# Three float32 half buffers instead of two, causal masks partly in place, row sums finished on ScalarE, twelve undivided score jobs

## The chip, the cores and the metric

The kernel runs on one core of one Trainium2 chip. The metric is device microseconds of one execution, lower being better; the program before took 1104.03 us (median of three runs, 1100.83 to 1107.71).

## What is computed

An attention with decay feeds two dense layers. Cut to what matters:

```python
B, H, S, D = 4, 8, 576, 64                     # attention: q, k, v; f in (0.8, 1)
scores = q @ k.T / 8 + (cum[:, None] - cum[None, :])   # cum = cumsum(log f)
attn   = softmax(where(causal, -1e9, scores))  # sum + 1e-9 in the divisor
x      = (attn @ v) as (2304 tokens, 512)
h = x @ w_in;  x = (h * clip(h + 3, 0, 6) / 6) @ w_out      # layer 1, 512 -> 2048 -> 512
h = x @ w_in2; x = where(h>=1, h, where(h<=-1, 0, (h+1)**2/4)) @ w_out2   # layer 2
```

The weights come in as 64-bit floats and are turned into float32 on the chip. Matrix products of the dense layers run in three passes on pairs (high part, low part) of a 32-bit format that TensorE reads in one pass.

## The kernel before

**Attention.** The 576 rows of a batch are cut into a first piece (rows 0 to 255) and a second one (256 to 575). `ORDER` lists the eight (batch, piece) in order, the first pieces of batches 0, 1 and 2 first. Each is worked in pairs of heads. For a first piece a pair is one job of kind `two` (two heads, two row tiles of 128); for a second piece it is two jobs of kind `one` (one head, row tiles 2 and 3) and one of kind `last` (64 rows of both heads). So jobs 0 to 11 are of kind `two`. A job goes through `u_load` (DMA from SyncE's queue, two jobs ahead), `u_split` (one job ahead), `u_scores` (scores on TensorE, then `softmax`: VectorE adds the decay and takes the row minimum, ScalarE takes the exponential and sums the row), `u_norm` (1/sum on VectorE, the product on VectorE or ScalarE), `u_trans` and `u_out`.

Jobs below `NATS` (8) are undivided: their q and k (tiles `kn`, `qn`) are loaded as they are and the scores are float32 matmuls over 64 rows (L376). The other jobs load q and k twice over (`kraw`, `qraw`, one buffer each), ScalarE rounds both (`kk`, `qh`), VectorE takes the remainders (L129: the lower half of `kk`, and `ql`), and the scores are two one-pass matmuls over 128 rows each (L386).

The causal mask: GpSimd's affine select (L312) writes the diagonal blocks of the decay tile `dec` into `dm`. A row tile that has columns left of its diagonal block takes two VectorE instructions per head, one on `dec` and one on `dm` that goes on from the first one's minimum.

**Dense layers.** Layer 1 works on token tiles of 256, as steps of one weight chunk each: `moe_h` (12 matmuls, L556, then `u` and `g` on ScalarE and VectorE) and, two steps later, `moe_o` (12 matmuls, L603). Attention pieces are woven between them by planned costs. Layer 2 runs after all attention (L556, L610).

**Weights.** `w_split` turns half a chunk of 64-bit words into float32 in a tile `wr` of tag "wr" (two buffers): ScalarE's L178 starts it, four VectorE instructions (L179, L183, L186, L189) finish it. For layer 1 it is then rounded into place (L196, L197); the halves of layer 2's 16 chunks (`wf16` to `wf31`) are written to memory by a DMA from GpSimd's queue (L194) and read back later. The output tiles `osb` of both layers (L617 to L630) are of the same tag "wr", so they share these buffers. The halves and their times are planned in `wq`; the instructions of each engine are then put in order by a scheduler, and each engine and each queue works in that order.

Of the kernel before, what the change touches and what calls it, by code (L numbers as in the profile page):

```python
# [8 lines left out]
F32 = mybir.dt.float32  # L9
F32R = mybir.dt.float32r  # L10
I32 = mybir.dt.int32
AF = mybir.ActivationFunctionType
ALU = mybir.AluOpType
# [3 lines left out]
P = 128  # L17
# [6 lines left out]
NEG = -8.0e9  # L24


QA = 256
# [1 line left out]
ORDER = ((0, 0), (1, 0), (2, 0), (0, 1), (1, 1), (3, 0), (2, 1), (3, 1))  # L29

DECS = 3
NATS = 8
NORMS = 12
FIRST = 10
EARLY = 6
# [39 lines left out]
def tile_kernel(  # L75
# [10 lines left out]
    nc = tc.nc  # L86
# [3 lines left out]
    moe = ctx.enter_context(tc.tile_pool(name="moe", bufs=2))  # L90
# [19 lines left out]
    att = att_cm.__enter__()  # L110
# [53 lines left out]
    def w_split(kind, c, half, s, raw):  # L164
        if kind == "parts":
            return
        if kind == "whole":
            lo = wsb[s][:, 1]
            rounded("a", wsb[s][:, 0], lo.bitcast(F32))
            rest("v", lo, lo.bitcast(F32), wsb[s][:, 0])  # L170
            return
        ks = slice(4 * half, 4 * half + 4)
        r = moe.tile([P, 4, P], F32, tag="wr", name="wr", bufs=2)
        rf = r.rearrange("p k n -> p (k n)")
        t = rf.bitcast(I32)
        lw, hw = raw[:, :, 0], raw[:, :, 1]

        nc.scalar.activation(out=rf, in_=hw.bitcast(F32), func=AF.Abs)  # L178
        nc.vector.tensor_scalar(  # L179
            out=rf, in0=rf, scalar1=2.0 ** -15, scalar2=122880.0,  # L180
            op0=ALU.max, op1=ALU.min,
        )
        nc.vector.tensor_scalar(  # L183
            out=t, in0=t, scalar1=5, scalar2=2, op0=ALU.logical_shift_left, op1=ALU.logical_shift_right
        )
        nc.vector.scalar_tensor_tensor(  # L186
            out=t, in0=hw, scalar=-1073741824, in1=t, op0=ALU.bitwise_and, op1=ALU.bitwise_or
        )
        nc.vector.scalar_tensor_tensor(  # L189
            out=t, in0=lw, scalar=29, in1=t,  # L190
            op0=ALU.logical_shift_right, op1=ALU.bitwise_or,
        )
        if s is None:
            nc.gpsimd.dma_start(out=wf[c][:, ks], in_=r)  # L194
        else:
            rounded("a", wsb[s][:, 0, ks], r)  # L196
            rest("v", wsb[s][:, 1, ks], r, wsb[s][:, 0, ks])  # L197
# [33 lines left out]
    def u_load(n):  # L231
        d = jobs[n]
        b, hs, kind, p = d["b"], d["hs"], d["kind"], d["p"]
        h, nh = hs[0], len(hs)
        r = b * H + h
        if kind == "last":

            d["dec"] = att.tile([P, S], F32, tag="dec", name="dec")
            nc.sync.dma_start(
                out=d["dec"], in_=ncum[r:r + 2, :].unsqueeze(1).to_broadcast([2, D, S])  # L240
            )
            return
        q0, nq, nk = (0, QA, QA) if kind == "two" else (QA, S - QA, S)
        d["nat"] = n < NATS
        if d["nat"]:

            kk = att.tile([P, S], F32, tag="kk", name="kn", bufs=3)
            qq = att.tile([P, 2 * QA], F32, tag="qh", name="qn", bufs=3)
            nc.sync.dma_start(out=kk[:, 0:nk], in_=k[b, h:h + 2, :, 0:nk].rearrange("h p n -> (h p) n"))
            for y in range(2):  # L250
                nc.sync.dma_start(
                    out=qq[y * D:(y + 1) * D, 0:nq], in_=q[b, h + y, y * D:(y + 1) * D, q0:q0 + nq]
                )
            d.update(kk=kk, qh=qq)
        else:
            kraw = att.tile([P, S], F32, tag="kraw", name="kraw", bufs=1)
            qraw = att.tile([P, 2 * QA], F32, tag="qraw", name="qraw", bufs=1)
            for y in range(2):
                nc.sync.dma_start(
                    out=kraw[y * D:(y + 1) * D, 0:nh * nk].rearrange("p (h n) -> p h n", h=nh),  # L260
                    in_=k[b, h:h + nh, :, 0:nk].rearrange("h p n -> p h n"),
                )
            if kind == "two":
                nc.sync.dma_start(
                    out=qraw.rearrange("p (h n) -> p h n", h=nh),
                    in_=q[b, h:h + nh, :, q0:q0 + nq].rearrange("h p n -> p h n"),
                )
            else:

                o = QA + W4 * (h % 2)  # L270
                nc.gpsimd.memset(qraw[:, S - o:S - o + W4], 0.0)
                nc.sync.dma_start(out=qraw[:, 0:QA], in_=q[b, h, :, q0:q0 + QA])
                nc.sync.dma_start(out=qraw[:, o:o + W4], in_=q[b, h, :, q0 + QA:S])
            d.update(kraw=kraw, qraw=qraw)
        w = nk if kind == "two" else 4 * P
        dec = att.tile([P, S], F32, tag="dec", name="dec")
        if n < DECS:
            t = bank("dc")
            for y in range(nh):
                ty = t[:, y * QA:(y + 1) * QA]  # L280
                for c in range(QA // P):
                    nc.tensor.matmul(
                        ty[:, c * P:], lhsT=lf0[:, c, h + y:h + y + 1].to_broadcast([P, P]), rhs=upper[:, 0:QA - c * P],
                        start=c == 0, stop=c == QA // P - 1,
                    )
            rounded("v", dec[:, 0:nh * nk], t[:, 0:nh * nk])
        else:
            nc.sync.dma_start(
                out=dec[:, 0:nh * w].rearrange("p (h n) -> p h n", h=nh),
                in_=ncum[r:r + nh, 0:w].unsqueeze(0).to_broadcast([P, nh, w]),  # L290
            )
        d.update(nk=nk, nq=nq, dec=dec, w=w)
        if n < 2:
            v_load(p)

    def u_split(n):
        d = jobs[n]
        kind, dec, nh = d["kind"], d["dec"], len(d["hs"])
        dm = att.tile([P, 2 * QA], F32, tag="dm", name="dm")
        if kind == "last":  # L300

            nc.gpsimd.affine_select(
                out=dm[:, 0:W4], in_=dec[:, 4 * P:S], compare_op=ALU.is_ge, fill=NEG, base=-D,
                pattern=[[-1, W4]], channel_multiplier=1,
            )
            nc.gpsimd.affine_select(
                out=dm[0:D, 0:W4], in_=dec[0:D, 4 * P:S], compare_op=ALU.is_ge, fill=NEG, base=0,
                pattern=[[-1, W4]], channel_multiplier=1,
            )
        else:  # L310
            q0, x = (0, 2 * QA) if kind == "two" else (QA, QA)
            nc.gpsimd.affine_select(  # L312
                out=dm[:, 0:x].rearrange("p (a n) -> p a n", n=P),
                in_=dec[:, q0:q0 + x].rearrange("p (a n) -> p a n", n=P),
                compare_op=ALU.is_ge, fill=NEG, base=0, pattern=[[0, x // P], [-1, P]], channel_multiplier=1,
            )
            if not d["nat"]:

                kraw, qraw = d.pop("kraw"), d.pop("qraw")
                kk = att.tile([P, S], F32R, tag="kk", name="kk", bufs=3)  # L320
                qh = att.tile([P, 2 * QA], F32R, tag="qh", name="qh", bufs=3)
                ql = att.tile([P, 2 * QA], F32R, tag="ql", name="ql", bufs=3)
                w, x = nh * d["nk"], 2 * QA if kind == "two" else QA + P
                rounded("a", kk[:, 0:w], kraw[:, 0:w])
                rest("v", kk[D:P, 0:w], kraw[D:P, 0:w], kk[D:P, 0:w])
                rounded("a", qh[:, 0:x], qraw[:, 0:x])
                rest("v", ql[:, 0:x], qraw[:, 0:x], qh[:, 0:x])
                d.update(kk=kk, qh=qh, ql=ql)
        d.update(dm=dm, prob={})
        d["sum"] = att.tile([P, 4], F32, tag="sum", name="sum")  # L330
        d["mx"] = att.tile([P, 8], F32, tag="mx", name="mx")
# [15 lines left out]
    def u_scores(n, i):  # L347
# [41 lines left out]
                    )  # L389
        for y in range(nh):  # L390
            t, zd = ts[y], y * 2 + j
            pieces = [(t[:, 0:w0], dec[:, y * nk:y * nk + w0], 0, w0)] if w0 else []
            pieces.append((t[:, w0:width], dm[:, zd * P:(zd + 1) * P], w0, width))
            softmax(d, zd, pr[:, y * width:(y + 1) * width], pieces)

    def u_norm(n):
# [2 lines left out]
        sm = d["sum"]  # L399
        rd = att.tile([P, 4], F32, tag="rd", name="rd")  # L400
        k = len(d["tiles"]) * len(d["hs"]) if d["kind"] != "last" else 1
        nc.vector.tensor_scalar(out=sm[:, 0:k], in0=sm[:, 0:k], scalar1=1e-9, scalar2=None, op0=ALU.add)
        nc.vector.reciprocal(out=rd[:, 0:k], in_=sm[:, 0:k])
        for j, i in enumerate(d["tiles"]):
            width = min(i * P + P, S)
# [176 lines left out]
    def moe_o(g):  # L582
# [31 lines left out]
                    )  # L614
        if n == NCH - 1:
            for k in range(len(acc[j])):
                o = moe.tile([P, 512], F32, tag="wr", name="osb", bufs=2)  # L617
                scale = 1.0 / 6.0 if layer == 0 else 1.0
                if k % 2:
                    nc.scalar.activation(out=o, in_=acc[j][k], func=AF.Copy, scale=scale)  # L620
# [224 lines left out]
```

## Time and profile before

| | us |
|---|---|
| median of 3 runs | 1104.03 |
| the profiled execution, its own time | 1102.54 |
| its span, first to last instruction | 1100.8 |
| TensorE matmul busy | 1031.1 (94%) |
| VectorE busy | 612.0 (56%) |
| ScalarE busy | 535.2 (49%) |
| GpSimd busy | 74.2 (7%) |
| 16 DMA engines, mean rate | 131 GB/s |
| mean granted TensorE clock | 0.973 |

The span has three stages: up to about 150 us the attention of the first pieces, the start of layer 1 and the conversion of its weights; up to about 560 us layer 1 with the rest of the attention and the conversion of layer 2's weights; then layer 2. Busy shares are means over a stage, so they are read by stretch. In the rows below, an engine's row gives start and length in us, and in square brackets how long the engine stood idle before it and what ended the wait.

### The profile page before, as it was taken

The page shows a single profiled execution, that of the slowest core. Times are in us where ns is not written, and L with a number is a line of the kernel's source. Part 1 is how long each engine was busy: PE and PEld are TensorE (multiplying, and loading weights), DVE is VectorE, ACT ScalarE, POOL GpSimd, SP SyncE. Part 2 cuts the span into 40 slices and gives each one's busy share as a digit, 9 for nine tenths or more (in the row PEclk, how much of TensorE's full clock was granted, in tenths as well). Part 3 has the DMA queues.
Part 4 walks back from the last instruction along what each step waited for, and adds up shares of the span by engine and source line. Part 5 has one row for each costly group of instructions (what it writes and reads, how often), then busy time and mean ns, then how long its engine had stood idle before and what let it go on. Part 6 is the DMA issues. An engine that isn't in the chain of part 4 may idle for free.

```text
span 1100.8 us, 18194 instructions
## 1 busy us (share of the span) xinstructions
PE 1031.1 (94%) x6556; PEld 898.3 (82%) x6556; DVE 612.0 (56%) x1702; ACT 535.2 (49%) x1266; POOL 74.2 (7%) x175
## 2 busy tenths in 40 slices
PE   6897999968889988998999999999999999999998
PEld 4576888968788878887999999888888888888887
DVE  8999985665677786777764426522422322322232
ACT  6877755455456655555554225623333333333343
POOL 2100000110011001111100100000100100000000
PEclk8798999989999999899999999999999999999999
DMA  8976781763486495684554115300200100010010
GB/s 242 306 233 184 222 286 52 238 219 114 144 322 189 147 323 171 191 300 132 173 173 190 68 40 181 126 1 1 77 1 1 58 20 0 20 39 1 1 40 19
DMA packets 69785, 144.20 MB, mean 131 GB/s; under 512 B 11584, under 2 KB 38720, under 8 KB 65600
## 3 DMA queue, kind: packets, MB, share of 16 engines
q1 hardware_dynamic: 67136, 134.66, 38.6%
q0 software_dynamic: 2560, 8.39, 1.9%
q8 instruction: 51, 0.84, 0.3%
q14 instruction: 38, 0.31, 0.1%
HBM read 116.74 MB, written 26.29 MB: 130 GB/s over the span
## 4 chain that ended last, share of the span: by engine, by line
PE 71%; DMA 12%; DVE 8%; issue 5%; ACT 2%; SPq 0%; POOL 0%; POOLq 0%; ACTq 0%; DVEq 0%
PE hp L556 31%; PE o L603 13%; PE o L610 10%; PE ps L610 8%; DMA dec<-ncum 4%; PE av L469 3%; DMA wf<-wr 3%; PE pt L427 3%; PE sc L386 2%; DMA qraw<-in_q 2%; DMA wraw<-in_w 1%; DVE prob L337 1%; PE sc L361 1%; DMA x2d<-osb 1%; DVE kk L129 1%
## 5 line engine op out<-in xcount | busy, mean ns | idle before, releaser
L603 PE MATMUL o<-g,w 128*128 128x256 f32 x1728 | 249.3, 289 | 23.8 <-ACT g L121 20.0
L556 PE MATMUL hp<-xt,w 128*128 128x256 f32 x1728 | 247.6, 290 | 5.3 <-ACT w L121 4.0
L603 PEld LDWEIGHTS o<-g,w 128*128 128x128 f32 x1728 | 224.1, 191 | 33.8 <-ACT g L121 23.2
L556 PEld LDWEIGHTS hp<-xt,w 128*128 128x128 f32 x1728 | 224.4, 193 | 11.9 <-ACT w L121 4.7
L556 PE MATMUL hp<-x,w 128*128 128x512 f32 (+1 forms) x960 | 211.4, 369 | 0.0
L556 PEld LDWEIGHTS hp<-x,w 128*128 128x128 f32 x960 | 169.1, 188 | 32.5
L567 DVE SCALAR_TENSOR_TENSOR u<-hp,u 128x512 f32<-128x512 f32 (+1 forms) x80 | 50.8, 637 | 197.5 <-ACT u L566 197.5
L121 ACT ACTIVATE g<-u 128x256 fp32r<-128x256 f32 (+1 forms) x224 | 105.9, 476 | 93.7 <-DVE u L567 55.3
L129 DVE TENSOR_TENSOR g<-u,g 128x256 fp32r<-128x256 f32 (+1 forms) x224 | 112.2, 503 | 68.9 <-ACT g L121 68.5
L565 ACT ACTIVATE u<-hp 128x512 f32<-128x512 f32 (+1 forms) x80 | 44.6, 557 | 177.9 <-PE hp L556 176.2
L610 PE MATMUL o<-w,g 128*128 128x512 f32 x480 | 124.9, 396 | 0.0
L610 PEld LDWEIGHTS o<-w,g 128*128 128x128 f32 x480 | 89.1, 188 | 19.9
L343 ACT ACTIVATE prob<-prob,mx 128x256 f32<-128x256 f32 (+4 forms) x144 | 83.4, 580 | 37.0 <-DVE mx L337 36.1
L610 PE MATMUL ps<-w,g 128*128 128x512 f32 x384 | 100.4, 396 | 0.0
L562 ACT ACTIVATE u<-hp 128x256 f32<-128x256 f32 x144 | 53.8, 378 | 75.3 <-PE hp L556 74.5
L563 DVE SCALAR_TENSOR_TENSOR u<-u,hp 128x256 f32<-128x256 f32 x144 | 59.4, 416 | 54.8 <-ACT u L562 54.6
L427 PE MATMUL pt<-ident,prob 128*128 128x128 f32 (+1 forms) x400 | 67.4, 289 | 22.9 <-DVE prob L412 19.6
L610 PEld LDWEIGHTS ps<-w,g 128*128 128x128 f32 x384 | 72.3, 188 | 17.4
L427 PEld LDWEIGHTS pt<-ident,prob 128*128 128x128 f32 (+1 forms) x400 | 48.5, 146 | 28.7 <-issue 14.2
L121 ACT ACTIVATE pt<-pt 128x512 f32<-128x512 f32 (+3 forms) x160 | 61.5, 432 | 18.9 <-PE pt L427 18.6
L178 ACT ACTIVATE wr<-wraw 128x512 f32<-128x512 f32 x64 | 42.9, 671 | 51.5 <-DMA wf<-wr 26.7
L337 DVE CUSTOM_DVE_ANT_0 prob<-sc,dec 128x128 f32<-128x128 f32 (+3 forms) x112 | 50.7, 457 | 23.9 <-PE sc L386 12.5
(75 smaller groups left out, 987.9 us busy)
## 6 DMA issues: line engine op xcount, KB each, us to landing
wraw<-in_w SPq DMA_DIRECT2D x64, 512.0 KB, 9.6
w<-wf SPq DMA_DIRECT2D x24, 1024.0 KB, 8.9
dec<-ncum SPq DMA_DIRECT2D x45, 256.0 KB, 7.7
kraw<-in_k SPq DMA_DIRECT2D x64, 144.0 KB, 4.8
wf<-w SPq DMA_DIRECT2D x8, 1024.0 KB
wf<-wr POOLq DMA_DIRECT2D x32, 256.0 KB, 6.1
w<-wf SPq DMA_DIRECT2D x16, 512.0 KB, 4.0
vv<-in_v SPq DMA_DIRECT2D x16, 320.0 KB, 6.3
```

Source lines behind the costliest of these rows:

```text
L121: nc.scalar.activation(out=out, in_=in_, func=AF.Copy)
L129: e.tensor_tensor(out=out, in0=in_, in1=hi.bitcast(F32), op=ALU.subtract)
L337: nc.vector.tensor_tensor_reduce(out=py[:, a:e], in0=s, in1=dc, scale=-0.125, scalar=mx[:, 2 * z:2 * z + 1] if x else 3.0e38, op0=ALU.add, ...
L343: nc.scalar.activation(out=py, in_=py, func=AF.Exp, scale=-1.0, bias=mx[:, 2 * z + x:2 * z + x + 1], accum_out=sm[:, z:z + 1],)
L427: nc.tensor.transpose(t[:nk, o:o + P], p[:, c:c + nk], ident)
L556: nc.tensor.matmul(hp, lhsT=ws[:, a, k], rhs=x[:, bb, 0:w], start=(k == 0 and a == 0 and bb == 0), stop=(k == KD - 1 and bb == 1),)
L562: nc.scalar.activation(out=u, in_=hp, func=AF.Relu, bias=3.0, scale=1.0)
L563: nc.vector.scalar_tensor_tensor(out=u, in0=u, scalar=6.0, in1=hp, op0=ALU.min, op1=ALU.mult)
L565: nc.scalar.activation(out=u, in_=hp, func=AF.Relu, bias=0.5, scale=0.5)
L567: nc.vector.scalar_tensor_tensor(out=u, in0=hp, scalar=1.0, in1=u, op0=ALU.max, op1=ALU.min)
L603: nc.tensor.matmul(o, lhsT=ws[:, a, KD + k], rhs=gg[:, bb], start=False, stop=(n == NCH - 1 and bb == 1 and k % 2 == 1),)
L610: nc.tensor.matmul(acc[j][k], lhsT=gg[:, bb, k * P:(k + 1) * P], rhs=ws[:, a, KD:2 * KD].rearrange("p k n -> p (k n)"), start=(n == 0 and ...
```

## The change

```diff
-NATS = 8
+NATS = 12
...
-        r = moe.tile([P, 4, P], F32, tag="wr", name="wr", bufs=2)
+        r = moe.tile([P, 4, P], F32, tag="wr", name="wr", bufs=3)
...
-            rounded("v", dec[:, 0:nh * nk], t[:, 0:nh * nk])
+            rounded("a", dec[:, 0:nh * nk], t[:, 0:nh * nk])
...
-        dm = att.tile([P, 2 * QA], F32, tag="dm", name="dm")
+        dm = att.tile([P, 2 * P], F32, tag="dm", name="dm")
...
-            q0, x = (0, 2 * QA) if kind == "two" else (QA, QA)
-            nc.gpsimd.affine_select(
-                out=dm[:, 0:x].rearrange("p (a n) -> p a n", n=P),
-                in_=dec[:, q0:q0 + x].rearrange("p (a n) -> p a n", n=P),
-                compare_op=ALU.is_ge, fill=NEG, base=0, pattern=[[0, x // P], [-1, P]], channel_multiplier=1,
-            )
+            q0, w = (0, d["nk"]) if kind == "two" else (QA, d["w"])
+            dh = dec[:, 0:nh * w].rearrange("p (h n) -> p h n", h=nh)
+            for o, x in ((dm[:, 0:nh * P].rearrange("p (h n) -> p h n", h=nh), q0), (dh[:, :, q0 + P:q0 + 2 * P], q0 + P)):
+                nc.gpsimd.affine_select(
+                    out=o, in_=dh[:, :, x:x + P], compare_op=ALU.is_ge, fill=NEG, base=0,
+                    pattern=[[0, nh], [-1, P]], channel_multiplier=1,
+                )
...
-            pieces = [(t[:, 0:w0], dec[:, y * nk:y * nk + w0], 0, w0)] if w0 else []
-            pieces.append((t[:, w0:width], dm[:, zd * P:(zd + 1) * P], w0, width))
+            if j:
+                pieces = [(t[:, 0:width], dec[:, y * nk:y * nk + width], 0, width)]
+            else:
+                pieces = [(t[:, 0:w0], dec[:, 0:w0], 0, w0)] if w0 else []
+                pieces.append((t[:, w0:width], dm[:, y * P:(y + 1) * P], w0, width))
...
-        nc.vector.tensor_scalar(out=sm[:, 0:k], in0=sm[:, 0:k], scalar1=1e-9, scalar2=None, op0=ALU.add)
+        nc.scalar.activation(out=sm[:, 0:k], in_=sm[:, 0:k], func=AF.Identity, bias=1e-9, scale=1.0)
...
-                o = moe.tile([P, 512], F32, tag="wr", name="osb", bufs=2)
+                o = moe.tile([P, 512], F32, tag="wr", name="osb", bufs=3)
```

Jobs 8 to 11 become undivided. The tag "wr" gets a third buffer of 2 KB a partition, and the two buffers of `dm` shrink from 2 KB to 1 KB each. The second row tile's mask is written in place into `dec`, so that its row tile is one VectorE instruction per head; the mask of a job becomes two selects of half the size. The decay of jobs 0 to 2 is copied out by ScalarE, and ScalarE adds 1e-9 to the sums.

Around the conversion of `wf16` to `wf18` (some 200 us into the program before) the change moves the starts of the halves on ScalarE. Before, between the last `pt` of the attention and the `kk` behind the fourth half, L178 is the start of a half, L562 is the dense layer's `u`, L343 the exponential:

```order
L178 ACTIVATE wr_3267<-wraw_3076 128x512
L562 ACTIVATE u_2848<-hp_2835 128x256
L121 ACTIVATE pt_2820<-pt_2822 128x2x256
L121 ACTIVATE pt_2820<-pt_2828 128x256
L121 ACTIVATE pt_2820<-pt_2828 128x128
L121 ACTIVATE g_2851<-u_2848 128x256
L178 ACTIVATE wr_3274<-wraw_3078 128x512
L343 ACTIVATE prob1_2854,sum_2648<-prob1_2854,mx_2649 128x512
```

Of the change, the same place (L567 is the old L562; wr_3269 is the old wr_3274, the second half of `wf17`, and wr_3510 the first half of `wf18`):

```order
L178 ACTIVATE wr_3269<-wraw_3071 128x512
L567 ACTIVATE u_2837<-hp_2824 128x256
L121 ACTIVATE xt_2752<-av_2738 128x64
L121 ACTIVATE g_2840<-u_2837 128x256
L178 ACTIVATE wr_3510<-wraw_3348 128x512
L121 ACTIVATE pt_2809<-pt_2811 128x2x256
L121 ACTIVATE pt_2809<-pt_2817 128x256
L121 ACTIVATE pt_2809<-pt_2817 128x128
```

The halves stand one half earlier against the dense layer and the attention: where the second half of `wf17` was started, the first of `wf18` is.

On GpSimd, the queue that also issues the writes to memory, the same place before (L302 and L306 are the masks of a `last` job, L271 clears a stretch of `qraw`):

```order
L271 MEMSET qraw_2919 128x64
L194 DMA wf16_98<-wr_2998 128x512
L302 AFFINE_SELECT dm_2717<-dec_2690 128x64
L306 AFFINE_SELECT dm_2717<-dec_2690 64x64
L194 DMA wf16_98<-wr_3005 128x512
L194 DMA wf17_99<-wr_3267 128x512
```

And of the change:

```order
L271 MEMSET qraw_2910 128x64
L194 DMA wf16_98<-wr_2992 128x512
L194 DMA wf16_98<-wr_2999 128x512
L194 DMA wf17_99<-wr_3262 128x512
L302 AFFINE_SELECT dm_2706<-dec_2679 128x64
L306 AFFINE_SELECT dm_2706<-dec_2679 64x64
L194 DMA wf17_99<-wr_3269 128x512
```

Two of the writes that stood behind the `last` job's mask now stand ahead of it.

On VectorE, the scores of job 7's second row tile (some 60 us into the program before), before, with the remainder of job 9's `kk` between:

```order
L337 ISA prob1_839,mx_582<-sc_842,dec_535 128x128
L337 ISA mx_582 128x1
L186 SCALAR_TENSOR_TENSOR wr_638<-wraw_562,wr_638 128x512
L129 TENSOR_TENSOR g_815<-u_812,g_815 128x256
L337 ISA prob1_839,mx_582<-sc_840,dm_577,mx_582 128x128
L337 ISA mx_582 128x1
L129 TENSOR_TENSOR kk_1067<-kraw_1009,kk_1067 64x512
L337 ISA prob1_839,mx_582<-sc_842,dm_577,mx_582 128x128
```

And of the change (L339 is the old L337):

```order
L339 ISA prob1_851,mx_593<-sc_852,dec_543 128x256
L339 ISA mx_593 128x1
L339 ISA prob1_851,mx_593<-sc_854,dec_543 128x256
L339 ISA mx_593 128x1
L129 TENSOR_TENSOR w5_120<-wr_647,w5_120 128x512
```

Each head's row tile is one instruction instead of two, and the remainders of `kk` and `ql` for job 9 are gone from the stream.

## Rows read from the trace of the kernel before

**Rows 1.** Windows: stretch, length, busy PE, PEld, DVE, ACT, POOL, clock, DMA, GB/s.

```profile
0.00:50.00 50.00, 37.03 (x157) 24.68 (x158) 42.88 (x163) 35.14 (x95) 7.85 (x18) 0.76 0.90 275
...
69.50:127.30 57.80, 47.31 (x355) 42.57 (x354) 57.05 (x161) 42.33 (x108) 3.67 (x7) 0.94 0.63 185
...
150.00:560.00 410.00, 372.41 (x2838) 336.82 (x2838) 283.84 (x906) 219.53 (x592) 46.03 (x120) 0.97 0.62 201
560.00:1100.80 540.80, 536.29 (x2932) 461.06 (x2930) 187.93 (x347) 205.67 (x391) 14.48 (x26) 1.00 0.14 48
```

**Rows 2.** VectorE in order of time, single instructions: start us, us, what.

```profile
62.22 0.17 DVE L402 TENSOR_SCALAR sum<-sum 128x4 f32<-128x4 f32 x1
...
83.06 0.34 DVE L337 CUSTOM_DVE_ANT_0 prob<-sc,dm,mx 128x128 f32<-128x128 f32 x1
...
83.33 0.28 DVE L337 CUSTOM_DVE_ANT_0 prob<-sc,dec 128x128 f32<-128x128 f32 x1
83.54 0.08 DVE L337 DVE_READ_ACCUMULATOR2_ANT mx<- 128x1 f32 x1
...
83.96 0.69 DVE L129 TENSOR_TENSOR ql<-qraw,qh 128x512 fp32r<-128x512 f32 x1
84.56 0.42 DVE L183 TENSOR_SCALAR wr<-wr 128x512 int32<-128x512 int32 x1
85.01 0.69 DVE L129 TENSOR_TENSOR kk<-kraw,kk 64x512 fp32r<-64x512 f32 x1
85.73 0.35 DVE L337 CUSTOM_DVE_ANT_0 prob<-sc,dm,mx 128x128 f32<-128x128 f32 x1
...
128.62 0.42 DVE L337 CUSTOM_DVE_ANT_0 prob<-sc,dec 128x256 f32<-128x256 f32 x1
128.97 0.08 DVE L337 DVE_READ_ACCUMULATOR2_ANT mx<- 128x1 f32 x1
```

**Rows 3.** Windows of the undivided scores (L376) alone: PE, PEld, clock, DMA, GB/s.

```profile
0.00:69.50 69.50, 17.35 (x64) 9.19 (x64) 0.83 0.89 274
```

**Rows 4.** Windows of the divided scores (L386) alone, same columns.

```profile
69.50:127.30 57.80, 4.89 (x33) 4.34 (x34) 0.94 0.63 185
```

**Rows 5.** GpSimd's select of 512 columns, VectorE at the same time, and 256-column selects by form.

```profile
72.71 0.64 POOL L312 TENSOR_SCALAR_AFFINE_SELECT dm<-dec 128x512 f32<-128x512 f32 x1 [7.36 <-DMA dec<-ncum]
...
72.80 1.09 DVE L129 TENSOR_TENSOR w<-wr,w 128x512 fp32r<-128x512 f32 x1
...
L312 POOL TENSOR_SCALAR_AFFINE_SELECT dm<-dec 128x256 f32<-128x256 f32 x32 | 15.1, 473 | 75.0 <-DMA dec<-ncum 53.4 <-DVE mx L337 13.8 <-DVE sum L402 7.7
```

**Rows 6.** SyncE's queue, GpSimd, ScalarE and TensorE around the longest idle time of TensorE.

```profile
203.20 0.54 SPq L239 DMA_DIRECT2D dec<-ncum  x1
...
215.44 0.23 POOL L302 TENSOR_SCALAR_AFFINE_SELECT dm<-dec 128x64 f32<-128x64 f32 x1 [7.79 <-DMA dec<-ncum]
...
216.44 0.56 POOL L194 DMA_DIRECT2D wf<-wr  x1
...
223.29 0.66 ACT L178 ACTIVATE wr<-wraw 128x512 f32<-128x512 f32 x1 [7.66 <-DMA wf<-wr]
...
229.41 0.66 PE L427 MATMUL pt<-ident,prob 128*128 128x128 f32 x2 [9.69 <-DVE prob L412]
```

**Rows 7.** Waits, 150 to 560 us: who waited for whom, us in total, times, longest.

```profile
ACT wr L178 <- DMA wf<-wr: 26.7, 9, 7.7
...
ACT wr L178 <- DMA x2d<-osb: 12.3, 5, 5.3
```

**Rows 8.** ScalarE and TensorE in order of time around 300 us.

```profile
294.47 0.66 ACT L178 ACTIVATE wr<-wraw 128x512 f32<-128x512 f32 x1 [5.33 <-DMA x2d<-osb]
...
302.87 0.67 ACT L178 ACTIVATE wr<-wraw 128x512 f32<-128x512 f32 x1 [4.78 <-DMA wf<-wr]
...
306.62 0.74 PE L603 MATMUL o<-g,w 128*128 128x256 f32 x4 [2.32 <-ACT g L121]
```

**Rows 9.** The chain that ended last, in order of time: start us, us, what.

```profile
284.77 9.61 DMA x2d<-osb
```

## The prediction

> **What bounds the kernel now.** I read the page's slices first, then busy time by stretch, then the waits, and last the single instructions around each long wait. By stretch there are three stages [rows 1]. From 560 us on TensorE is busy 536.3 of 540.8 us: nothing the change touches can shorten that, it can only start earlier. From 150 to 560 us TensorE is busy 372.4 of 410 us, VectorE 283.8: TensorE bounds, with 37.6 us of holes in it. Up to 150 us VectorE bounds: from 69.5 to 127.3 us it is busy 57.05 of 57.8 us, with TensorE idle 10.5 us. In the first 50 us VectorE is busy 42.9 and the DMA engines 0.90 of the time, so there it bounds only in part.
>
> The largest hole, 9.69 us, shows the second stage's trouble [rows 6]. The decay of a `last` job is issued on SyncE's queue at 203.20, and its mask starts on GpSimd only at 215.44, when it has landed. The write of the second half of `wf16` stands behind that mask in GpSimd's order and is issued at 216.44. ScalarE's next half needs that half's buffer, one of two, and waits 7.66 us, to 223.29. Everything behind it on ScalarE (exponentials, `u`, `g`) waits along, then VectorE's probabilities, then TensorE, to 229.41. Over the stage ScalarE waits 26.7 us in nine such places and 12.3 us in five places for an output tile's write, which holds the same buffers [rows 7].
>
> **The change part by part, first stage.** Of busy VectorE instructions I count start to start, since they overlap.
> - Undivided jobs 8 to 11: the remainders go, 0.60 us for `ql` (83.96 to 84.56) and 0.72 for `kk` (85.01 to 85.73) [rows 2], 1.32 x 4 = 5.3 us. ScalarE loses two roundings a job; that is off the bound.
> - One instruction per head instead of two in the second row tile: 0.21 (83.33 to 83.54) + 0.27 (83.06 to 83.33) become 0.35 (128.62 to 128.97) [rows 2]: 0.13 a head, two heads, 12 jobs: 3.1 us. Later jobs save as much each, but VectorE is not the bound there.
> - The sums: the addition lasts 0.17 us [rows 2], of which a part overlaps; between nothing and that I take half, 12 x 0.08 = 1.0 us. On ScalarE, busy 42.3 of 57.8 us [rows 1], the addition is a new small instruction. No row shows one of four columns; it lies between nothing and the 0.17 us that VectorE's lasts plus a wait for the exponential's own sum. ScalarE's 15 us of idle time cover 12 of them. If that cover were gone, it would be 2 us.
> - The three decay copies of 512 columns: at the 0.60 us of `ql`, the same width, 1.8 us. They lie in the first 20 us, where VectorE is not full; I count half, 0.9.
>
> Together 10.3 us, at most 12. Against it stand two things.
>
> TensorE works longer: eight undivided jobs took 17.35 us, 2.2 a job [rows 3], while the divided scores show 33 matmuls in 4.89 us, so 1.2 a job of eight [rows 4]; the first stretch had the lower clock, 0.83 against 0.94, so this is rather too much. Four jobs cost 4 us, at 69.5 to 127.3 us, where 10.5 us are idle. They are hidden by VectorE's bound; without it they would cost the 4 us. With 51 us of TensorE work in a stretch some 4 us shorter, TensorE is nearly full, and I take off 1 us.
>
> GpSimd's masks hold VectorE up. During a select (72.71, 0.64 us) VectorE's remainder of a weight, 512 columns, took 1.09 us where `ql` of the same size took 0.69 [rows 2, 5]: 0.40 us lost. Two selects of 256 columns, 0.47 us each [rows 5], replace one; a second instruction may be hit (0.4 us more a job) or none. I take half, 0.2 x 12 = 2.4 us.
>
> The Trainium skill, page "SBUF — State Buffer", section "SBUF: two separate sides", says more: VectorE (two-port modes, or two SBUF inputs) and GpSimd share a port pair as an exclusive lock, and the later one is blocked for the other's whole instruction. The trace agrees on the kind of thing, with 0.40 us, but not on the whole 0.64; what the whole length would give stands with the rivals.
>
> First stage: 10.3 - 1 - 2.4 = 6.9, taken as **7 us** (bounds 0 and 12).
>
> **Second stage: the third buffer.** Scheduling moves with it: in the order rows above, the halves stand one half earlier on ScalarE. So the buffer does not simply wait in reserve, and I go place by place.
> - The 9.69 us hole. After the change the second half of `wf17` needs the buffer of the first half of `wf16`, whose write was never behind the mask. On GpSimd the writes of both halves of `wf16` and the first of `wf17` now stand ahead of that mask. What held ScalarE is gone for the three halves that follow. What is late next is the write of `wf17`'s second half, and its buffer is wanted only at the next tile's end. I take 8.5 us off, leaving 1.2.
> - The wait at 302.87 (4.78 us, hole 2.32 [rows 8]): the half ahead of it no longer waits for the output tiles, so its write goes out earlier: 1.5 us.
> - The wait at 294.47 (5.33 us [rows 8]) is for an output tile's write, 9.61 us long [rows 9]. The third buffer serves one half, but the order puts a third half in the same place, which then waits for the same write: nothing.
> - The other seven waits of the nine add up to 14.3 us, mostly without a hole as long behind them: 2 us.
> Second stage: **12 us** (bounds 0, if each wait forms anew one half later, and 9.7 + 2.3 + 14.3 = 26).
>
> The second select of the later jobs, GpSimd being busy 46 of 410 us [rows 1], is made a job ahead and costs nothing; where `dec` lands late it is on the path, with at most the 0.47 us of a whole 256-column select. The last stage has its output tiles' third buffer too, but no hole to close.
>
> **Sum.** 1102.54 - 7 - 12 = 1083.5 us for the profiled execution; the median of the runs lies 1.5 us above it, so **1085 us**.
>
> **Rivals.**
> - *The waits form anew.* The scheduler has spent the third buffer by starting halves earlier, and the landing times (9.61 us for an output tile) are what they were. For it: the order rows, and five waits for output tiles. Against it: the masks no longer stand ahead of two of the writes. Only the first stage gains: 1104 - 7 = 1097 us. Chance 0.20.
> - *TensorE takes the first stage.* With 4 us more work and dependences at every tile, it may not follow VectorE: 7 becomes 0, and only the 12 us stay: 1092 us. Chance 0.14.
> - *The masks hold VectorE for their whole length.* Two selects would take 2 x 0.47 = 0.94 us of VectorE's time where one took 0.40: 0.54 x 12 = 6.5 us in place of my 2.4, so the 7 become 2.9 and the time 1089 us. For it: the one row; against it: that row shows 0.40 of 0.64 us. Chance 0.10. (The exclusive lock of the Trainium skill's page "SBUF — State Buffer" is this case.)
> - *Slower: the third half at each tile's end.* Two output tiles and three halves now come together; the third half on ScalarE stands ahead of `u` and waits for the second output tile. Before, the second half waited 5.33 us of a 9.61 us write. If the third meets the whole of it, that is 4.3 us more at each of five tile ends, 21 us, with the other waits as they were: 1104 - 7 + 21 = 1118 us. It decides as soon as a tile end costs more than 7 / 5 = 1.4 us in addition. Against it: the write starts when the accumulation ends and lands at the same time either way. Chance 0.14.
>
> **How the numbers follow.** The forecast has 0.42. Its own range, 1071 to 1095, comes from gains of 12 + 21 us (the second: both named holes and two thirds of the 14.3) and of 9 us in all. For eight in ten the range takes in 1097 and stops at no change, and below it goes to 12 + 23: **1069 to 1104 us**. Measurements of this kernel spread by 0.6%, so 1% (11 us) is about what can be told from no change. Below 1093 lie most of the forecast and of the 1089 case, half of the 1092 case and a little of the 1097 one: 0.60. Above 1115 lies most of the last rival: 0.13. Within 1%: 0.27.
>
> **What would show it.** Right: by stretch, the first stage's work ends some 7 us earlier, with VectorE still above 0.95 of 69 to 120 us; no hole near 9 us around 200 to 220 us, and ScalarE's waits for `wf` writes well below 26.7 us. Wrong: waits of ScalarE for output tiles above 12.3 us, TensorE's idle time from 150 to 560 us still near 37 us, or VectorE's instructions stretched beside GpSimd's masks. The prediction falls if a new hole of several us opens behind a queue that I have not followed, SyncE's above all, where decay tiles and weights share the way.

## The result, and the profile after

| | before | changed |
|---|---|---|
| median, us | 1104.96 (4 runs) | 1087.89 (4 runs, 1084.11 to 1090.63) |
| ratio | 1 | 0.9857, 95% interval 0.9819 to 0.9894 |
| the profiled execution, its own time, us | 1102.54 | 1090.63 |
| its span, us | 1100.8 | 1088.9 |
| TensorE busy in it, us | 1031.1 | 1041.6 |
| TensorE idle in it (span minus busy), us | 69.7 | 47.3 |

The changed kernel is faster by 1.4% (1.1 to 1.8%). 1085 us was forecast, 1087.89 measured. Run again later, as a1 below, the same file gave 0.9841 (0.9811 to 0.987). The profiled execution is the slowest of its four, so a part of the difference is missing in it. TensorE is idle 22.4 us less, but busy 10.5 us longer.

Windows of the changed kernel (stretch, length, busy us of PE, PEld, DVE, ACT, POOL, clock, DMA share, GB/s), beside [rows 1]:

```profile
0.00:50.00 50.00, 39.66 (x158) 26.32 (x159) 40.82 (x136) 37.44 (x107) 10.56 (x26) 0.73 0.87 279
69.50:127.30 57.80, 53.92 (x350) 45.65 (x351) 52.99 (x143) 41.06 (x110) 10.13 (x10) 0.88 0.65 198
150.00:560.00 410.00, 382.24 (x2885) 347.23 (x2884) 273.23 (x801) 230.59 (x652) 56.36 (x156) 0.96 0.63 199
560.00:1088.90 528.90, 524.43 (x2840) 449.68 (x2838) 178.59 (x315) 199.21 (x375) 13.68 (x22) 1.00 0.14 46
```

From 69.5 to 127.3 us TensorE is the busier engine in this execution: 53.92 us, VectorE 52.99; before it was 47.31 and 57.05. In a1 it is not: at a granted clock of 1.00 instead of 0.88 TensorE is busy 52.78 us there, VectorE 56.23. From 150 to 560 us TensorE's idle time fell from 37.6 to 27.8 us. The last stage is as it was, and starts earlier.

GpSimd and TensorE of the changed kernel, in order of time, where the 9.69 us hole of [rows 6] was:

```profile
201.31 0.55 POOL L194 DMA_DIRECT2D wf<-wr  x1 [2.76 <-DVE wr L189]
203.82 0.55 POOL L194 DMA_DIRECT2D wf<-wr  x1 [1.97 <-DVE wr L189]
214.57 0.23 POOL L302 TENSOR_SCALAR_AFFINE_SELECT dm<-dec 128x64 f32<-128x64 f32 x1 [10.20 <-DMA dec<-ncum]
...
215.11 0.69 POOL L194 DMA_DIRECT2D wf<-wr  x1
...
215.73 0.44 PE L432 MATMUL pt<-ident,prob 128*128 128x128 f32 x2 [1.93 <-DVE prob L417]
```

The mask comes as late as before (214.57), but two writes stand ahead of it now, and TensorE waits 1.93 us. At a later tile end, 450 us, the same thing has formed anew (SyncE's queue, GpSimd, ScalarE, TensorE):

```profile
437.81 0.54 SPq L239 DMA_DIRECT2D dec<-ncum  x1
...
449.45 0.24 POOL L302 TENSOR_SCALAR_AFFINE_SELECT dm<-dec 128x64 f32<-128x64 f32 x1 [15.70 <-DMA dec<-ncum]
...
450.24 1.63 POOL L194 DMA_DIRECT2D wf<-wr  x3 [0.24 <-issue]
...
456.56 0.66 ACT L178 ACTIVATE wr<-wraw 128x512 f32<-128x512 f32 x1 [10.79 <-DMA wf<-wr]
...
458.47 1.86 PE L561 MATMUL hp<-xt,w 128*128 128x256 f32 x7 [6.95 <-ACT pt L121]
```

All three buffers' writes now stand behind this mask, and ScalarE waits 10.79 us for the first of them. In a1 the hole stands at the same place in the order and is 4.17 us long. Waits of the changed kernel, 150 to 560 us, beside [rows 7]:

```profile
ACT wr L178 <- DMA wf<-wr: 18.6, 5, 10.8
...
ACT wr L178 <- DMA x2d<-osb: 11.4, 6, 6.5
```

### The profile page after: what moved, and what is told of

It is laid out like the page before. It is cut to its first block, busy times and chain, and to the rows that moved or that the text cites. A ratio compares the mean times of both kernels' runs of the same rounds, so it can differ in the third digit from the quotient of the medians.

```text
span 1088.9 us, 18059 instructions
## 1 busy us (share of the span) xinstructions
PE 1041.6 (96%) x6556; PEld 906.5 (83%) x6556; DVE 584.1 (54%) x1499; ACT 538.7 (49%) x1325; POOL 95.9 (9%) x223
## 4 chain that ended last, share of the span: by engine, by line
PE 74%; DMA 15%; DVE 5%; ACT 3%; issue 2%; SPq 1%; POOL 0%; DVEq 0%; ACTq 0%; POOLq 0%
PE hp L561 33%; PE o L608 13%; PE o L615 10%; PE ps L615 8%; DMA dec<-ncum 8%; PE av L474 3%; DMA wraw<-in_w 3%; PE pt L432 2%; PE sc L388 2%; DMA kraw<-in_k 2%; DMA wf<-wr 1%; DVE prob L339 1%; PE sc L363 1%; DMA qraw<-in_q 1%; PE sc L378 1%
## 5 line engine op out<-in xcount | busy, mean ns | idle before, releaser
L561 PE MATMUL hp<-xt,w 128*128 128x256 f32 x1728 | 250.8, 293 | 13.4 <-ACT pt L121 6.9
L561 PEld LDWEIGHTS hp<-xt,w 128*128 128x128 f32 x1728 | 227.8, 196 | 23.6 <-ACT pt L121 7.5
L608 PEld LDWEIGHTS o<-g,w 128*128 128x128 f32 x1728 | 226.0, 192 | 22.6 <-ACT g L121 11.2
L567 ACT ACTIVATE u<-hp 128x256 f32<-128x256 f32 x144 | 54.0, 378 | 73.2 <-PE hp L561 70.7
L615 PEld LDWEIGHTS ps<-w,g 128*128 128x128 f32 x384 | 72.3, 188 | 17.4
L339 DVE CUSTOM_DVE_ANT_0 prob<-sc,dec 128x256 f32<-128x256 f32 (+1 forms) x112 | 59.3, 534 | 41.1 <-DMA dec<-ncum 18.4
L121 ACT ACTIVATE pt<-pt 128x512 f32<-128x512 f32 (+3 forms) x160 | 61.1, 433 | 16.9 <-PE pt L432 16.5
L178 ACT ACTIVATE wr<-wraw 128x512 f32<-128x512 f32 x64 | 42.9, 672 | 45.6 <-DMA wf<-wr 18.6
L474 PE MATMUL av<-pt,vv 128*64 128x320 f32 (+3 forms) x448 | 55.8, 381 | 3.2 <-ACT pt L121 3.2
```

Source lines behind the costliest of these rows:

```text
L121: nc.scalar.activation(out=out, in_=in_, func=AF.Copy)
L339: nc.vector.tensor_tensor_reduce(out=py[:, a:e], in0=s, in1=dc, scale=-0.125, scalar=mx[:, 2 * z:2 * z + 1] if x else 3.0e38, op0=ALU.add, ...
L474: nc.tensor.matmul(t[y * D:(y + 1) * D, o:nq], lhsT=vv[:nk, y, c], rhs=rhs, start=c == 0, stop=c == nkc - 1,)
L561: nc.tensor.matmul(hp, lhsT=ws[:, a, k], rhs=x[:, bb, 0:w], start=(k == 0 and a == 0 and bb == 0), stop=(k == KD - 1 and bb == 1),)
L567: nc.scalar.activation(out=u, in_=hp, func=AF.Relu, bias=3.0, scale=1.0)
L608: nc.tensor.matmul(o, lhsT=ws[:, a, KD + k], rhs=gg[:, bb], start=False, stop=(n == NCH - 1 and bb == 1 and k % 2 == 1),)
```

## The experiments

The theory at the start: the third buffer closes the 9.69 us hole (some 12 us), and VectorE's relief shortens the first stage (some 7 us). Rivals: the waits form anew one half later; TensorE takes the first stage; the masks hold VectorE up. Each version is compared with the kernel before, run on the same chip. The versions a, b and c ran on three different chips, so a difference between two letters is less sure than one within a letter: the changed kernel itself gave 0.9857 and 0.9841. "Idle" is TensorE's in the profiled execution, a window's length minus its busy time. A profiled execution can lie some 4 us off the median, in b2 7.5 us, so the ratio decides and the idle times only say where. In the traces a1 and c2 keep ScalarE's order of instructions; in the other versions the scheduler lays it anew, so a difference there is that of the edit together with the order that it led to.

| version | median us | ratio, 95% interval | idle 0 to 150 | idle 150 to 560 |
|---|---|---|---|---|
| before | 1103.45 (a), 1102.4 (b), 1102.5 (c) | 1 | 27.6 | 37.6 |
| changed kernel again (a1) | 1085.45 | 0.9841, 0.9811 to 0.987 | 13.0 | 28.6 |
| changed, two buffers (a2) | 1092.7 | 0.9908, 0.9883 to 0.9934 | 20.9 | 33.3 |
| changed, eight undivided jobs (a3) | 1086.05 | 0.9847, 0.9816 to 0.9877 | 21.4 | 23.6 |
| a3 without sums and copies moved (a4) | 1090.97 | 0.9891, 0.9865 to 0.9917 | 26.5 | 22.2 |
| changed, writes on SyncE's queue (b1) | 1086.03 | 0.987, 0.9845 to 0.9896 | 15.0 | 29.1 |
| changed, copies back on VectorE (b2) | 1094.25 | 0.9922, 0.9897 to 0.9946 | 20.6 | 26.8 |
| before, twelve undivided jobs (b3) | 1095.38 | 0.9961, 0.993 to 0.9993 | 17.4 | 32.1 |
| before, masks in place (b4) | 1091.57 | 0.9915, 0.9885 to 0.9944 | 24.4 | 25.8 |
| b4, two pieces a head (c1) | 1105.51 | 1.0025, 1.0003 to 1.0047 | 28.0 | 38.2 |
| before, two selects (c2) | 1102.39 | 0.9999, 0.9977 to 1.002 | 24.8 | 34.7 |
| changed, writes on ScalarE's queue (c3) | 1081.64 | 0.9818, 0.9795 to 0.9841 | 16.0 | 26.0 |
| changed, sums back on VectorE (c4) | 1085.71 | 0.9854, 0.9833 to 0.9876 | 23.4 | 24.9 |

**Parts taken back or done alone (a1 to a4).** a1 has no edit.

> The changed kernel unchanged, for a second profile beside the others. Theory (VectorE's work and the third buffer each gave some 6 us by the first profile's steps): 1084 to 1092 us, and in the profile the same holes as before at about 283 us and 451 us and the GpSimd select of 7 us at about 87 us, since the order is fixed. Rival (these are accidents of one execution): the holes and the long select lie elsewhere or are gone, with the time as it was.

```diff
 # a2, of the changed kernel
-        r = moe.tile([P, 4, P], F32, tag="wr", name="wr", bufs=3)
+        r = moe.tile([P, 4, P], F32, tag="wr", name="wr", bufs=2)
-                o = moe.tile([P, 512], F32, tag="wr", name="osb", bufs=3)
+                o = moe.tile([P, 512], F32, tag="wr", name="osb", bufs=2)
 # a3, of the changed kernel
-NATS = 12
+NATS = 8
 # a4, of a3
-            rounded("a", dec[:, 0:nh * nk], t[:, 0:nh * nk])
+            rounded("v", dec[:, 0:nh * nk], t[:, 0:nh * nk])
-        nc.scalar.activation(out=sm[:, 0:k], in_=sm[:, 0:k], func=AF.Identity, bias=1e-9, scale=1.0)
+        nc.vector.tensor_scalar(out=sm[:, 0:k], in0=sm[:, 0:k], scalar1=1e-9, scalar2=None, op0=ALU.add)
```

> The change without the third buffer of the tag wr. Theory (half of the gain is the buffer's): 1092 to 1100 us, with a hole of TensorE of 5 us or more near 200 to 230 us and ScalarE's waits for writes of wf back to 20 us and more. Rival (the waits form anew anyway, the gain is VectorE's alone): 1086 to 1091 us.

> The change with eight undivided jobs, as before. Theory (the remainders of jobs 8 to 11 are half of VectorE's saving in the first stage, 5.3 of 10.3 us): 1090 to 1095 us, the loss being there by step 24 of the dense layer. Rival (TensorE's 4 us more work and the low clock took that back): 1085 to 1089 us, or faster than the whole change.

> Only the masks in place and the third buffer, with eight undivided jobs and sums and decay copies on VectorE. Theory (3.1 us for the instructions of the softmax less what GpSimd holds up, and the buffer's 6 to 10): 1092 to 1099 us. Rival (the gain is the buffer's nearly alone): 1086 to 1091; other rival (nearly all is the undivided jobs' and sums'): 1100 to 1106 us.

The third buffer is worth 0.9908 - 0.9841, 7.4 us, not 12. It acts where it was said to: without it ScalarE's waits for `wf` writes are 28.2 us in seven places (16.3 in five in a1), and a hole of 5.60 us stands at 219 us. The undivided jobs 8 to 11, the largest of VectorE's terms, are worth nothing that can be told (0.9847 against 0.9841). The sums and copies, priced at 1.9 us, are worth 0.9891 - 0.9847, 4.9 us. And a4, masks and buffer alone, already has most of the gain: 12 us. That lies where the rival "nearly all the buffer's" had it; a2 and the next version tell against that rival.

**Masks alone (b4), and with two pieces again (c1).** b4 is the kernel before with the three edits of the masks and of `pieces`. c1 takes the merged instruction back:

```diff
             if j:
-                pieces = [(t[:, 0:width], dec[:, y * nk:y * nk + width], 0, width)]
+                pieces = [(t[:, 0:w0], dec[:, y * nk:y * nk + w0], 0, w0), (t[:, w0:width], dec[:, y * nk + w0:y * nk + width], w0, width)]
```

> The kernel before with the masks in place and the smaller mask buffer alone: two half buffers, eight undivided jobs, sums and copies on VectorE. Prediction on record for this part: 3.1 us saved in VectorE's pieces, 2.4 lost beside GpSimd's selects, so within 1 us of 1104: 1103 to 1104 us. Rival: half of the 12.5 us by which masks and third buffer together gained (1090.97 us) are the masks', since the single pieces also shorten the second stage's path from score to exponential: 1097 to 1099 us. Second rival: the selects that are stretched to 7.1 us beside VectorE's run cost more than the pieces give: 1106 us or more.

> The kernel before with the masks in place and the smaller mask buffer, but with two VectorE instructions per head in the second row tile, as before (both read the decay tile). The version with one instruction took 0.9915 of the time of before. Theory A: the gain is VectorE's saved instructions (some 137 fewer), which shorten the path from score to exponential in the second stage as well: without them the time is that of before or 2 us more, for the second select (1102 to 1105 us). Theory B: the gain does not hang on VectorE's time, but on how the scheduler lays the same ScalarE waits against TensorE's work: then it need not go, 1090 to 1098 us, with the order of the instructions deciding and TensorE's idle time from 150 to 560 us below 32 us.

Masks in place alone gain 9.4 us (6.2 to 12.7), more than either range on record, and none of it is left without the merged instruction: c1 is 0.25% slower than before. The window from 150 to 560 us of b4, and from its waits those of TensorE:

```profile
150.00:560.00 410.00, 384.19 (x2929) 349.26 (x2930) 281.45 (x855) 227.85 (x608) 55.74 (x156) 0.97 0.65 206
...
PE o L608 <- ACT g L121: 18.5, 8, 4.6
PE pt L432 <- DVE prob L417: 3.7, 4, 1.5
```

The same two views of c1:

```profile
150.00:560.00 410.00, 371.79 (x2830) 337.34 (x2828) 284.05 (x914) 222.31 (x594) 54.34 (x151) 0.96 0.63 201
...
PE pt L432 <- DVE prob L417: 18.9, 5, 8.0
PE o L608 <- ACT g L121: 10.1, 5, 4.2
```

With two pieces TensorE waits 18.9 us for the probabilities that VectorE hands on; with one, 3.7 us. That looks as if VectorE's time were what counts. But two holes make up 14.8 of the 18.9 us, and behind each of them stands ScalarE (ScalarE, VectorE, TensorE of c1, twice):

```profile
226.28 0.66 ACT L178 ACTIVATE wr<-wraw 128x512 f32<-128x512 f32 x1 [5.59 <-DMA wf<-wr]
226.97 0.43 DVE L179 TENSOR_SCALAR wr<-wr 128x512 f32<-128x512 f32 x1 [5.19 <-ACT wr L178]
232.11 0.66 PE L432 MATMUL pt<-ident,prob 128*128 128x128 f32 x2 [8.04 <-DVE prob L417]
...
308.61 0.66 ACT L178 ACTIVATE wr<-wraw 128x512 f32<-128x512 f32 x1 [9.22 <-DMA wf<-wr]
309.31 0.43 DVE L179 TENSOR_SCALAR wr<-wr 128x512 f32<-128x512 f32 x1 [6.66 <-ACT wr L178]
311.88 0.69 PE L432 MATMUL pt<-ident,prob 128*128 128x128 f32 x2 [6.71 <-DVE prob L417]
```

ScalarE waits for a write, VectorE stands idle with it (5.19 and 6.66 us), and only then come the exponential, the product and the transposition. Of the instructions that VectorE runs from the end of its wait up to that product, the merge saves none. So these holes are not VectorE's own time. ScalarE's waits for `wf` are not fewer in b4 either (27.8 us in nine places, 29.2 in nine in c1). In b4, GpSimd, ScalarE and TensorE around 215 us:

```profile
211.69 0.24 POOL L302 TENSOR_SCALAR_AFFINE_SELECT dm<-dec 128x64 f32<-128x64 f32 x1 [14.37 <-DMA dec<-ncum]
...
212.27 1.29 POOL L194 DMA_DIRECT2D wf<-wr  x2
...
218.78 0.66 ACT L178 ACTIVATE wr<-wraw 128x512 f32<-128x512 f32 x1 [7.56 <-DMA wf<-wr]
...
221.71 2.78 PE L608 MATMUL o<-g,w 128*128 128x256 f32 x12 [4.03 <-ACT g L121]
```

ScalarE waits 7.56 us behind the same late mask, as in [rows 6] (7.66), but TensorE's hole is 4.03 us instead of 9.69. Here TensorE's next work is a dense step that needs `g`, and it goes on 2.9 us after ScalarE's wait ends; in c1 it is a transposition that needs the whole softmax, 5.8 us after the wait at the first hole and 3.3 at the second, where the wait itself is the longest (9.22 us). So the traces speak for the order that the scheduler laid, in the second stage at least. How much of the 12 us between c1 and b4 is time saved and how much order is not settled, since no version holds the order fixed.

**The second select alone (c2).** The kernel before, its select cut into two of half the size; every other engine's order stays row for row.

```diff
-            nc.gpsimd.affine_select(out=dm[:, 0:x]..., in_=dec[:, q0:q0 + x]...)
+            for z in (0, x // 2):
+                nc.gpsimd.affine_select(out=dm[:, z:z + x // 2]..., in_=dec[:, q0 + z:q0 + z + x // 2]...)
```

> The kernel before, whose one select of a job into the mask buffer is cut into two of half the size; every other engine's order stays as it was, row for row. It measures the price of the second select alone. Prediction on record: 0.2 us a job for twelve jobs of the first stage, 2.4 us: 1104 to 1106 us. Rival on record (VectorE held up for the whole length of each select): 6.5 us, 1108 to 1111 us. Third: GpSimd gives way and VectorE loses nothing: 1102 to 1104 us.

0.9999: the second select costs nothing that can be told, 2.2 us at the most. The rival of 6.5 us falls, and the 2.4 us of the sum lie just outside the interval. With its order kept, the kernel keeps its hole as well (TensorE of c2):

```profile
231.29 0.66 PE L428 MATMUL pt<-ident,prob 128*128 128x128 f32 x2 [9.65 <-DVE prob L413]
```

**Undivided jobs alone (b3).** The kernel before with `NATS = 12`.

> The kernel before with twelve undivided jobs in place of eight, nothing else. Prediction on record: 5.3 us of VectorE's time saved, some 1 us lost to TensorE, so 1098 to 1101 us beside 1104. Rival, after the version of the changed kernel with eight (0.6 us above it, nothing that can be told): the divided remainders cost nothing also where VectorE has more to do, because TensorE's own work in 69.5 to 127.3 us (4 us more for four jobs) takes back what VectorE gives: 1103 to 1105 us.

4.3 us (0.8 to 7.7), which is what was forecast for the term (5.3 - 1), within a wide interval. From 0 to 150 us TensorE's idle time falls by 10.2 us, and its work grows: over the whole program 1037.2 us busy against 1031.1. In the changed kernel the same edit brings no time that can be told: from a3 to a1 TensorE's idle time up to 150 us falls by 8.4 us, but from 150 to 560 us it grows by 5.0, and its work by 3.5 (1033.1 to 1036.6), each read from one execution.

**Copies and sums apart (b2, c4).** The two edits of a4 above, one at a time, on the changed kernel.

> The changed kernel, with the three 512-column copies of decay tiles (line 286) back on VectorE, the sums' additions still on ScalarE. It splits the 4.9 us by which the version with eight undivided jobs (1086.05 us) is below the version with neither sums nor copies moved (1090.97 us). Theory A: the copies are it, since on VectorE they stand behind other work in the first 50 us, and the first scores and masks start later: 1089 to 1091 us, and the first stage's activations some 4 to 8 us later at the first steps. Theory B: the sums are it (the additions keep VectorE's order tight over the whole first stage): within 1.5 us of the changed kernel's 1085.45 us.

> The changed kernel with the additions to the sums back on VectorE and the decay copies on ScalarE. With the copies back on VectorE the time was 0.9922 of before, the changed kernel's 0.9841. Theory A (the copies at the start are worth 5 us or more, the sums about nothing): within 1.5 us of the changed kernel, 1084 to 1087 us. Theory B (the sums are worth 1 us, as predicted, or more): 1087 us or more. Theory C (the sums on ScalarE cost, since VectorE's reciprocal then waits for ScalarE, 4.3 us in the second stage): 1080 to 1083 us, and this version would be the best.

With three copies of 512 columns in the first 16 us back on VectorE the kernel is 0.9922 - 0.9841, 8.9 us, slower, with intervals apart; against b1 (0.987), which ran on the same chip and is otherwise as fast as a1, it is 5.7 us. Both theories on record had less. The sums are worth 1.4 us, which can't be told from none. The copies themselves are hardly shorter on ScalarE (0.58 us there, 0.68 on VectorE), and they let nothing start earlier: the first transposition is at 18.79 us in b2, at 18.61 in the changed kernel and at 19.12 in a1. So the gain comes behind them, and the order is laid anew here as well. The first 150 us hold 7.6 us more idle time of TensorE in b2 than in a1. b2's profiled execution was the quickest of its own (1086.72 us), so its trace shows less than the median, and what carries the gain stays open.

**The write's queue (b1, c3).** Of the changed kernel, the write of a half:

```diff
-            nc.gpsimd.dma_start(out=wf[c][:, ks], in_=r)
+            nc.sync.dma_start(out=wf[c][:, ks], in_=r)      # b1
+            nc.scalar.dma_start(out=wf[c][:, ks], in_=r)    # c3
```

> The changed kernel, with the writes of the rounded halves of a weight (line 194, wf from wr) issued on SyncE's queue in place of GpSimd's. Theory: what holds ScalarE at a tile end is still the mask that stands ahead of such a write in GpSimd's order (in the changed kernel the mask started 15.7 us late at 449.45 us, three writes behind it, and ScalarE waited 10.8 us). Then ScalarE's waits for a wf write fall from 18.6 us in five places to under 8, there is no hole of TensorE above 4 us between 430 and 470 us, and the time is some 4 to 7 us below the changed kernel: 1079 to 1082 us. Rival: the waits are the landing time of the writes (6.3 us each), whichever queue issues them: waits as before, 1084 to 1088 us. Second rival: the writes now hold up the weights and decay tiles that stand behind them on SyncE's queue, since SyncE has to wait for ScalarE and VectorE before it issues one: 1090 us or more, with longer waits for decay tiles and weights.

b1 misses: ScalarE's waits grew to 27.6 us in ten places, and the time is that of the changed kernel. SyncE's queue and ScalarE of b1 around 450 us:

```profile
442.10 0.33 SPq L194 DMA_DIRECT2D wf<-wr  x1
...
444.84 0.33 SPq L160 DMA_DIRECT2D w<-wf  x1
445.26 0.43 SPq L194 DMA_DIRECT2D wf<-wr  x1
...
454.56 0.66 ACT L178 ACTIVATE wr<-wraw 128x512 f32<-128x512 f32 x1 [6.69 <-DMA wf<-wr]
```

No mask stands ahead of the writes, but they share a queue with weight loads of up to 1 MB, and ScalarE waits 6.69 us for one of them all the same. The slowest write took 11.2 us from issue to landing in b1, 8.3 in the changed kernel; that the loads held it up is likely, but not shown.

> The changed kernel, with the writes of the rounded halves issued on ScalarE's queue. On SyncE's queue (1086.03 us) they no longer stood behind the mask, but behind weight loads: a write issued at 442.10 us came back only near 454.5. ScalarE's queue carries nothing else. Theory: then neither a mask nor a load stands ahead of a write, ScalarE's waits for wf writes fall below 10 us and the time is 1078 to 1083 us. Rival: ScalarE, which issues the write in its order, now waits for VectorE to finish the half, and what it saves in one wait it pays in the other: 1084 to 1090 us.

c3 has the lowest time of all: 1081.64 us. GpSimd, ScalarE and its queue at the same place, and ScalarE's waits from 150 to 560 us:

```profile
439.74 0.24 POOL L302 TENSOR_SCALAR_AFFINE_SELECT dm<-dec 128x64 f32<-128x64 f32 x1 [14.76 <-DMA dec<-ncum]
...
434.87 0.33 ACTq L194 DMA_DIRECT2D wf<-wr  x1
441.15 0.66 ACT L178 ACTIVATE wr<-wraw 128x512 f32<-128x512 f32 x1 [4.91 <-DMA wf<-wr]
442.63 0.33 ACTq L194 DMA_DIRECT2D wf<-wr  x1
...
ACT wr L178 <- DMA wf<-wr: 13.0, 6, 4.9
```

The mask is as late as ever (14.76 us), and nothing waits behind it: the longest wait of ScalarE for a write is 4.91 us, not 10.8, and TensorE's longest hole between 430 and 470 us is 1.80 us. The waits add up to 13.0 us, not to less than 10. c3's interval touches that of the changed kernel (0.9795 to 0.9841 against 0.9811 to 0.987), and the two ran on different chips, so a gain of some 2.5 us over it is not shown.

## Why the prediction held, step by step

The total came out (19 us forecast, 17 measured), and the range held, since errors of both signs met in it. The direction was reasoned; that the size came so near was luck.

- **The merged pieces: mis-sized, the worst step.** "Later jobs save as much each, but VectorE is not the bound there" priced them at nothing beyond the first stage. They go with about 12 us (c1 against b4). Of TensorE's idle time 3.6 us goes up to 150 us, near the 3.1 of the sum, and 12.4 us from 150 to 560 us (38.2 to 25.8), which was priced at nothing. That VectorE is not the bound there is not refuted: it stood idle ahead of c1's two largest holes. What the step left out is that fewer instructions lead to another order, and that the order decides what TensorE waits for behind a wait of ScalarE.
- **The second select: mis-sized.** 2.4 us taken off, nothing measured (c2). The one row on which it stood, 1.09 us instead of 0.69 [rows 2, 5], is there, but the added select does not add to the time.
- **Undivided jobs: the size was right for the edit alone** (4.3 us in b3), but the terms were added up as if they didn't share a bound. With copies, sums and pieces moved, VectorE's saved remainders still take 8.4 us off TensorE's idle time up to 150 us, and it is lost again in longer work of TensorE (3.5 us) and in new idle time later (5.0 us). The rival "TensorE takes the first stage" named the first of these; its 4 us of longer work is near that.
- **The decay copies: mis-sized,** 0.9 us against 5.7 to 8.9. They were priced by their length and by VectorE's share at the start; what they are worth beyond that has no explanation yet. The sums: 1.0 against 1.4, within what can be told.
- **The third buffer: the mechanism was right, the size too large.** The named hole went (9.69 to 1.93 us), for the reason given: writes ahead of the mask. The step "its buffer is wanted only at the next tile's end" holds at 215 us. At 450 us, a place that the sum did not go through, three writes stand behind one mask and a hole of 6.95 us opens (4.17 in a1). So the rival "the waits form anew" came true in one place, and 12 us became 7.4. Without the other edits (b4 to a4, on two chips) the buffer is worth 2.6 us, which can't be told from none, though ScalarE's waits for `wf` fall there from 27.8 to 9.6 us, so most of these waits cost TensorE little.
- **The waits for output tiles** were priced at nothing: 12.3 us in five became 11.4 in six. The longest grew from 5.3 to 6.5 us. The slower rival needed more than 1.4 us at each tile end and falls.
- **The signs named:** no hole near 9 us at 200 to 220 us, right. Waits for `wf` "well below 26.7": 18.6, in one place longer than before. VectorE above 0.95 of the stretch from 69 us: 0.92 in this execution, 0.97 in a1. VectorE stretched beside masks: not seen at the longest select (below).

The parts don't add up: masks 9.4 and undivided jobs 4.3, each put into the kernel before, and copies 8.9 and third buffer 7.4, each taken out of the changed one, are 30 us; the change gave 17. Put in one after the other, it goes 9.4 us with the masks (b4), 12.0 with the buffer (a4), 16.9 with sums and copies (a3), 17.5 with the undivided jobs (a1).

## What to carry over

Follow a wait to its far end before you price an edit by it: TensorE's waits for VectorE's probabilities began with ScalarE waiting for a write. Where a scheduler lays the order, an edit changes the order of all engines, and that can outweigh the time of the instructions it saves: here 12.4 us of idle time went where nothing was forecast. Where edits relieve the same bound, test each alone and in company before adding their gains. A write that frees a buffer is best kept from queues in which something waits ahead of it: on a queue of its own the longest wait for one fell from 10.8 to 4.91 us, though the gain in time is not shown.

## What the runs showed of the hardware

GpSimd's in-place select of 256 columns, 0.40 us long at 75.00 us, shows a length of 7.14 us at 86.70 us in the changed kernel. GpSimd and VectorE, in order of time:

```profile
75.00 0.40 POOL L315 TENSOR_SCALAR_AFFINE_SELECT dec<-dec 128x256 f32<-128x256 f32 x1
...
86.70 7.14 POOL L315 TENSOR_SCALAR_AFFINE_SELECT dec<-dec 128x256 f32<-128x256 f32 x1
...
86.72 0.68 DVE L129 TENSOR_TENSOR w<-wr,w 128x512 fp32r<-128x512 f32 x1
...
93.15 0.42 DVE L179 TENSOR_SCALAR wr<-wr 128x512 f32<-128x512 f32 x1
93.85 0.42 DVE L339 CUSTOM_DVE_ANT_0 prob<-sc,dec 128x256 f32<-128x256 f32 x1 [0.29 <-POOL dec L315]
```

VectorE ran without a gap from 86.72 to 93.57 us, at its usual lengths (0.68 us), and then waited 0.29 us for the select. In a1 and c3 the select is as long (7.13 us), beside the same run of VectorE. The end of such a record is rough: in a1 the VectorE instruction that reads the tile starts at 92.46 us, the record ends at 92.82. The Trainium skill, page "SBUF — State Buffer", section "SBUF: two separate sides", says that, for certain operations, whichever of the two starts first holds a shared port pair for its instruction and the other is blocked. The trace agrees only in part: the one that seems to wait is GpSimd, though its record starts first (86.70), and over a whole run of VectorE's instructions; VectorE loses 0.29 us.

Between 80 and 100 us TensorE's clock fell in the profiled execution and not in a1 (windows of the changed kernel):

```profile
80.00:90.00 10.00, 7.32 (x50) 6.20 (x51) 10.00 (x31) 7.41 (x21) 3.75 (x2) 0.90 0.74 218
90.00:100.00 10.00, 10.00 (x40) 8.14 (x38) 8.62 (x20) 6.14 (x13) 3.83 (x1) 0.50 0.57 172
```

Behind 10 us in which TensorE was idle 2.7 us, with the granted clock at 0.90, the clock was 0.50 (1.2 GHz) for the next 10 us, and 40 matmuls filled them. In a1, idle 2.7 us in the same stretch (7.26 busy), it stayed at 1.00 (2.4 GHz) and did 59. Over the whole program the two profiled executions of one kernel differ by 5.0 us of TensorE's busy time (1041.6 and 1036.6); this stretch is not all of it, since up to 69.5 us it is a1 that has the lower clock (0.75 against 0.80).
